# Decay attention and a sticky-routed MoE on Trainium2: two q loads, one low half of weights and the token gathers change places

## The chip, the cores and the metric

The kernel runs on one core of one Trainium2 chip. The metric is the device time of one execution in microseconds (us); the time of a kernel is the median of its runs. One more execution was taken by the hardware profiler, and all rows below come from that one.

## The reference, cut to what matters

Attention with a decay, 8 batches of 8 heads, 576 positions, 64 wide, and then a mixture of 8 experts in which a token either takes its own best expert or keeps the expert of the token before it.

```
def _attn_ref(q, k, v, f):                      # B, H, S, D = 8, 8, 576, 64
    scores = scale * np.matmul(q, k.transpose(0, 1, 3, 2))
    cum = np.cumsum(np.log(np.clip(f, 0.0001, 1.0)), axis=-1)
    decay = cum[:, :, :, None] - cum[:, :, None, :]
    scores = np.where(causal, -1000000000.0, scores + decay)
    attn = softmax(scores)
    return np.matmul(attn, v)

def _moe_ref(x, w_gate, w_local, w1, w2):       # x: 8 x 576 x 512, w1: 8 x 512 x 1024, w2: 8 x 1024 x 512
...
            fresh_e = int(np.argmax(logits[b, s]))
            e = fresh_e if s == 0 or local_gate[b, s] < 0.5 else prev_e
...
            h = np.maximum(x[b, s] @ w1[e], 0.0)
            out[b, s] = p[e] * (h @ w2[e])
```

All is float32. The kernel multiplies in fp16 with each operand split into a high and a low half (x = high + low), and three products in place of one: high by high, high by low, low by high.

## The kernel before, in words

**Engines.** TensorE (PE) multiplies, VectorE (DVE) and ScalarE (ACT) read its results from PSUM and split them, GpSimd (POOL) splits inputs, adds weights and issues the transfers with lists of indices (gathers and scatters), SyncE (SP) issues all other transfers, in the order of the program. Each engine works its instructions off in order.

**Attention.** Eight batches come one after the other, each in 25 units of up to 512 columns. A unit is: scores st on PE (L894, a product over 128 partitions of Ak and Aq and one over 70 of KB and QB, the latter carrying the decay), the negated maximum nm on DVE (L905), the exponentials P on ACT (L925), transposes pt of P on PE (L940), their high half ph on ACT (L945) and low half pl on DVE (L949), and the product with v on PE (xp, L919). Four heads' columns are divided by their sums at L980 (reciprocal rs) and L984.

While a batch is computed, the next ones are prepared. SP loads q and k into ldq and ldk (load_main, L209: two transfers of 512 KB for each; load_last, L216: the last 64 positions). POOL splits them to fp16, t16q and t16k (hi_lo, L359 the high, L363 the low half), PE turns the pieces (L429, 8 at a time), ACT or DVE write them to Aq or Ak, and SP copies the other half of each into QB and KB (L409 and L406, the last 64 positions at L413). What is issued when is set by lists of moves at the head of the file: each list has a due time of a planner, and when it is reached, its moves are issued in the order that they stand in. ORDC holds two lists, due at 47000 and 56000 of the planner's time:

```
ORDC = moves_of("q:2"), moves_of("k:2 q:L k:L")
...
        elif a == "2":
            new_load(2, b)
            for C in range(2):
                load_main(2, b, C, 0, H)
        elif a == "L":
            load_last(2, b)
```

The copies KB<-Ak of the second batch stand between the two on SP's queue.

**MoE.** Two fixed stages of experts come first, then six ranked stages r = 0 to 5 (the function `ranked`, and the loop that calls it), which take the experts by their number of tokens, with room for 608, 592, 576, 576, 544 and 480. A stage is a sequence of steps, and a list of (step, function) pairs says beside which step of PE everything else is issued. Steps 0 to 27 are W1 by seven products in place of eight (`seven`): products zb and zd (L1848), a kept copy et on ACT (L1855), sums y and zd on DVE (L1861), then the high half hh on ACT (L1865) and the low half hl on DVE (L1866). From step 28 on come the tiles of W2, four steps each, 24 matmuls of 512 columns (L1805). Where more than 64 tokens are left over 128s (96 in r=0 and r=5, 80 in r=1), that tile is turned: its 96 matmuls are as narrow as its tokens (L1800), and it comes second, in r=5 first; a smaller rest is a half tile at the end (L1809). Each tile's result is multiplied by the gate into a tile o of three buffers on ACT (L1748; a half tile at L1776) and scattered by POOL (L1750), with a drain of POOL ahead of the scatter (L1749).

Beside these steps stand, among others:
- the second half of the weights of the stage's own expert, cut into high halves on ACT (L2118: uh, or wh where the buffer has that name) and low halves on DVE (L2120: ul, wl), at the steps in the table UC, a pair (high, low) for each 128 rows;
- the sums of the next expert's weights on POOL (L2132 to L2141);
- the loads of the expert after it on SP, as buffers come free (L2090, L2093);
- the tokens of stage r+2, for r = 0 to 3: gathers xg<-xs of 128 tokens each on POOL (L1695) at the first step of XA, and their transposes xT<-xg on SP (L1700) at the second.

```
UC = (0, 0), (1, 1), (2, 2), (22, 23), (24, 25), (26, 27)
XA = (32, 42)
...
        todo += [call(y, M.second, (i + 2) // 2, i % 2, low) for i, x in enumerate(UC) for low, y in enumerate(x)]
...
            todo += tokens_at(r + 2, XA)
```

Of the kernel before, what the change touches and what calls it, by code (L numbers as in the profile page):

```python
# [38 lines left out]
def moves_of(d):  # L39
    return [tuple(x.split(":")) for x in d.split()]  # L40
# [5 lines left out]
ORD2 = moves_of(':lm q:M k:m k:M :sp :at 0:R 1:R :lv q:a k:a')  # L46
ORDA = moves_of("q0:P k:M 0:V 1:V k:ag")
ORDB = moves_of("q:ag q:G0 2:V q1:P k0:P k1:P 3:V q:G1 k:G0 :vl :Vl k:G1 :iv v0:P")
ORDC = moves_of("q:2"), moves_of("k:2 q:L k:L")


LI = (16, 18)
# [46 lines left out]
SEVEN = (1, 1, 1, 1, 1, 1)  # L99
WP = (28, 30, 32, 36)  # L100
LA = (6, 7, 8, 9), (10, 11, 12, 13)
UC = (0, 0), (1, 1), (2, 2), (22, 23), (24, 25), (26, 27)
UB = 45
UN = (5, 24, 29)
XA = (32, 42)
WC = (28, 29, 29, 30, 31, 31, 38, 38)
TA = (28, 36, 37, 44)
FA = (9, 10, 11, 12, 13, 14, 15, 16), (17, 18, 19, 20), (1, 4, 7, 9), (17, 22), (15, 16, 17, 18), 22, (20, 26)
# [8 lines left out]
def kernel(  # L117
# [586 lines left out]
    def due_c(i):  # L704
        for x in ORDC[i]:
            moves(x)
# [1795 lines left out]
    def call(x, f, *args):  # L2502
        return x, lambda: f(*args)
# [13 lines left out]
    def tokens_at(r, at):  # L2517
        if r >= NR:
            return []

        def gathers():
            Xs[r] = tokens_of(r)
            whole(both(*Xs[r][1]))

        return [(at[0], gathers), (at[1], lambda: whole(both(*Xs[r][2])))]
# [17 lines left out]
    for r in range(NR):  # L2543
        M, xc, todo = N, xn, []
        todo += [call(y, M.second, (i + 2) // 2, i % 2, low) for i, x in enumerate(UC) for low, y in enumerate(x)]
        if r + 1 < NR:
# [3 lines left out]
            todo += [call(0, N.load, ST)] + [call(x, N.load) for x in UN]  # L2550
            todo += tokens_at(r + 2, XA)
            if SEVEN[r + 1]:
# [100 lines left out]
```

## Time and profile before

| | us |
|---|---|
| median of 3 runs | 783.45 |
| runs, lowest to highest | 780.44 to 786.8 |
| the profiled execution, its own time | 784.89 |
| its span | 783.1 |
| PE busy in it | 738.4 |

The mean granted clock of PE over the span is 0.989 of full speed. A group's rows say: the start in us from the span's start, how long it took, engine, line, operation, what is written and from what, shapes, and how many instructions the row stands for; in brackets how long the engine stood idle before it, and what ended that. "issue" there means that the engine waited for nothing that the profile shows. SPq is SP's queue of transfers issued. Rows of a window give, for a stretch, the busy time and count of each engine, the granted clock, the busy share of the DMA engines and what they moved.

### The profile page before, as it was taken

Reading aid. Unit: us, or ns where it says so; the run is one execution under the profiler, and the core shown is the slowest. Engines: PE = TensorE matmul, PEld = TensorE weight load, DVE = VectorE, ACT = ScalarE, POOL = GpSimd, SP = SyncE. Lnnn points to the kernel's source line nnn. Section 1 sums busy time; section 2 is a strip of 40 time slices with the busy share of each in tenths; the row PEclk is TensorE's granted clock in tenths of the full one; section 3 lists DMA queues with packets and bytes.
Section 4 is the critical chain, followed back from the end, with each engine's and each line's share of the span. In section 5 each row is a group of like instructions: output and inputs, shape, how many; then the busy total and the mean of one; then the engine's idle time right before and its main releaser. Section 6 shows DMA issues by size and latency. Waiting matters only on the chain.

```text
span 783.1 us, 21924 instructions
## 1 busy us (share of the span) xinstructions
PE 738.4 (94%) x8661; PEld 537.7 (69%) x8661; DVE 599.3 (77%) x1295; ACT 508.3 (65%) x1006; POOL 469.0 (60%) x521
## 2 busy tenths in 40 slices
PE   5898999999999998989799999999999999999996
PEld 3686888887878877878554565575664747576682
DVE  7886888898898989899648856669577695968650
ACT  7796788988878978868524315366464665657441
POOL 6879969395879849837672365436282553634201
PEclk9999999999999999999999999999999999999999
DMA  7559879798786968155794776497737486561201
GB/s 186 139 124 201 177 160 185 168 148 208 149 188 129 177 155 154 37 98 192 179 244 154 189 198 119 116 237 155 232 102 163 151 178 209 151 224 64 73 3 50
DMA packets 189659, 120.75 MB, mean 154 GB/s; under 512 B 129397, under 2 KB 165511, under 8 KB 189532
## 3 DMA queue, kind: packets, MB, share of 16 engines
q1 hardware_dynamic: 183473, 100.19, 55.4%
q0 software_dynamic: 6080, 19.13, 8.1%
q8 instruction: 69, 1.13, 0.6%
q14 instruction: 37, 0.30, 0.1%
HBM read 72.25 MB, written 19.32 MB: 117 GB/s over the span
## 4 chain that ended last, share of the span: by engine, by line
PE 61%; DVE 12%; issue 12%; ACT 6%; POOL 4%; POOLq 2%; DMA 1%; ACTq 0%; DVEq 0%
PE y L1805 15%; PE pt L940 9%; PE st L894 7%; PE xp L919 6%; PE z L1763 6%; PE zb L1848 5%; DVE nm L905 4%; DVE pl L949 3%; PE st L429 3%; POOLq L1749 2%; PE zd L1848 2%; ACT ph L945 2%; ACT P L925 2%; PE yt L1848 1%; PE y L1800 1%
## 5 line engine op out<-in xcount | busy, mean ns | idle before, releaser
L925 ACT ACTIVATE P<-st,nm 128x512 f32<-128x512 f32 (+3 forms) x288 | 152.8, 588 | 27.6 <-DVE nm L905 25.5
L945 ACT CAST ph<-pt 128x512 f16<-128x512 f32 (+1 forms) x200 | 115.4, 588 | 38.1 <-PE pt L940 35.1
L905 DVE TENSOR_REDUCE nm<-st 128x1 f32<-128x512 f32 (+4 forms) x264 | 133.1, 540 | 7.2 <-PE st L901 4.7
L949 DVE TENSOR_TENSOR pl<-pt,ph 128x512 f16<-128x512 f32 (+1 forms) x165 | 109.1, 668 | 24.8 <-ACT ph L945 22.6
L940 PE MATMUL pt<-ident,P 128*128 128x128 f32 x784 | 121.9, 281 | 5.0 <-DVE pl L949 2.1
L1750 POOL DMA_INDIRECT out_dram<-o,ranki x26 | 30.2, 1162 | 135.4 <-ACT o L1748 59.3
L940 PEld LDWEIGHTS pt<-ident,P 128*128 128x128 f32 x784 | 84.3, 142 | 21.3 <-DVE pl L949 3.7
L919 PE MATMUL xp<-VH,pl 128*128 128x65 f16 (+1 forms) x960 | 90.2, 195 | 6.3 <-DVE pl L949 5.7
L919 PE MATMUL xp<-VH,ph 128*128 128x65 f16 (+1 forms) x960 | 91.6, 196 | 3.0 <-ACT ph L945 2.0
L919 PEld LDWEIGHTS <-ph 128*128 128x128 f16 (+1 forms) x1920 | 83.8, 103 | 11.7 <-issue 4.5
L1805 PEld LDWEIGHTS <-hh 128*128 128x128 f16 x528 | 51.4, 98 | 58.5
L919 PE MATMUL xp<-VL,ph 128*128 128x65 f16 (+1 forms) x960 | 91.0, 195 | 0.0
L894 PE MATMUL st<-Ak,Aq 128*128 128x256 f16 (+4 forms) x448 | 77.6, 284 | 4.4 <-ACT P L925 2.4
L919 PEld LDWEIGHTS <-pl 128*128 128x128 f16 (+1 forms) x960 | 75.4, 103 | 7.6 <-DVE pl L949 6.7
L894 PE MATMUL st<-KB,QB 70*128 70x256 f16 (+4 forms) x448 | 77.1, 280 | 2.2 <-DMA KB<-Ak 2.2
L1805 PE MATMUL y<-uh,hh 128*128 128x512 f16 x168 | 63.7, 379 | 0.0
L1805 PE MATMUL y<-uh,hl 128*128 128x512 f16 x168 | 63.7, 379 | 0.0
L1805 PE MATMUL y<-ul,hh 128*128 128x512 f16 x168 | 63.7, 379 | 0.0
L1763 PE MATMUL z<-xT,wh 128*128 128x384 f16 (+2 forms) x256 | 55.8, 309 | 1.0 <-DVE hl L1738 0.9
L1805 PEld LDWEIGHTS <-hl 128*128 128x128 f16 x264 | 25.8, 98 | 30.7
L1848 PEld LDWEIGHTS <-wh 128*128 128x128 f16 x384 | 37.5, 98 | 10.9 <-issue 2.5
L1748 ACT ACTIVATE o<-y,rank 128x512 f32<-128x512 f32 x23 | 15.7, 683 | 44.1 <-PE y L1805 31.4
(441 smaller groups left out, 2014.0 us busy)
## 6 DMA issues: line engine op xcount, KB each, us to landing
stg<-in_moe_w_dram SPq DMA_DIRECT2D x64, 512.0 KB
xs<-xr SPq DMA_DIRECT2D x16, 512.0 KB
ldq<-in_q_dram SPq DMA_DIRECT2D x14, 512.0 KB
ldk<-in_k_dram SPq DMA_DIRECT2D x14, 512.0 KB
ldv<-in_v_dram SPq DMA_DIRECT2D x28, 256.0 KB
QB<-Aq SPq DMA_DIRECT2D x15, 256.0 KB
KB<-Ak SPq DMA_DIRECT2D x15, 256.0 KB
ldv<-in_v_dram SPq DMA_DIRECT2D x20, 64.0 KB
```

The costliest lines, as they stand in the source:

```text
L429: nc.tensor.transpose(U["pt"][:, a], t16[:, 8 * j + a], ident16)
L894: nc.tensor.matmul(st[p0:p0 + m, co:co + n], lhsT=queries(lq, kk, h, c), rhs=rhs, start=(ps == 0 and first and co == col), stop=(ps == 1), ...
L905: nc.vector.tensor_reduce(dst, src, axis=AX.X, op=ALU.max, negate=True)
L919: nc.tensor.matmul(xo, lhsT=a[:, c0:c0 + m], rhs=w[:, vi, :], start=False, stop=(i == n - 1 and jj == 2), skip_group_check=True)
L925: nc.scalar.activation(P[:, c0:c1].rearrange("p (k x r) -> p k r x", r=2, x=64), st[:, c0:c1].rearrange("p (k r x) -> p k r x", r=2, x=64) ...
L940: nc.tensor.matmul(U["pt"][:, i * 128:(i + 1) * 128], lhsT=P[:, i * 128:(i + 1) * 128], rhs=ident, is_transpose=True, start=(i == 0), stop ...
L945: nc.scalar.copy(U["ph"][:, :cols], U["pt"][:, :cols])
L949: nc.vector.tensor_tensor(U["pl"][:, :cols], U["pt"][:, :cols], U["ph"][:, :cols], ALU.subtract)
L1750: nc.gpsimd.indirect_dma_start(out=outf if EX.get("over") else next_out(), out_offset=bass.IndirectOffsetOnAxis(ap=scat(t)[0:m], axis=0), ...
L1763: nc.tensor.matmul(z[:, a, 0:wd], lhsT=w[:, d, fc * 128:(fc + 1) * 128], rhs=xT[:, x, a * wd:(a + 1) * wd], start=(i == 0), stop=(i == len ...
L1805: nc.tensor.matmul(y[0:m], lhsT=a[:, fc, t * 128:t * 128 + m], rhs=u[:, fc], start=(i == 0), stop=(i == len(prods) - 1))
L1848: nc.tensor.matmul(out, lhsT=w, rhs=v, start=(start and i == 0), stop=(i == len(ops) - 1), skip_group_check=True)
```

## The change

Three lines of tables:

```
-ORDC = moves_of("q:2"), moves_of("k:2 q:L k:L")
+ORDC = moves_of(""), moves_of("q:2 k:2 q:L k:L")
...
-UC = (0, 0), (1, 1), (2, 2), (22, 23), (24, 25), (26, 27)
+UC = (0, 0), (1, 1), (2, 2), (22, 24), (24, 25), (26, 27)
...
-XA = (32, 42)
+XA = (37, 44)
```

The first moves the loads of q of the third batch from the list of 47000 to the head of the list of 56000. On SP, in the attention of the first batch, this stands in the program (QB and KB are the second batch's):

```order
 L409 DMA QB_109<-Aq 64x2x1024 x2
 L413 DMA QB_109<-Aq 64x512
-L209 DMA ldq<-in_q_dram 128x8x128 x2
 L406 DMA KB_111<-Ak 64x2048 x2
 L413 DMA KB_111<-Ak 64x512
+L209 DMA ldq<-in_q_dram 128x8x128 x2
 L209 DMA ldk<-in_k_dram 128x8x128 x2
 L216 DMA ldq<-in_q_dram 64x4x64 x2
```

The two loads of q went behind three copies of k; nothing else on SP changed place.

The second moves one low half (L2120, the fourth pair of UC) by one step in each ranked stage. On DVE, in stage r=1, near the end of W1:

```order
 L1866 SCALAR_TENSOR_TENSOR hl<-zb,hh 128x296
 L1866 SCALAR_TENSOR_TENSOR hl<-yt,hh 128x296
-L2120 SCALAR_TENSOR_TENSOR ul<-stg,uh 128x512
 L1861 TENSOR_TENSOR y<-zd,et 128x296
+L2120 SCALAR_TENSOR_TENSOR ul<-stg,uh 128x512
 L1861 TENSOR_TENSOR zd<-zd,et 128x296
 L1866 SCALAR_TENSOR_TENSOR hl<-y,hh 128x296
```

The low half went behind the first of two sums; the other five stages read alike, with other widths.

The third moves the gathers of stages 0 to 3 from step 32 to step 37, and their transposes from step 42 to step 44. On POOL, in stage r=0 (s and stg are the sums of the next expert's weights, out_dram the scatters):

```order
 L2136 TENSOR_TENSOR s_11172<-stg 128x512
 L2141 TENSOR_TENSOR s_11186<-stg,s_11172 128x512 x2
+L1750 DMA out_dram<-o,ranki 4608x512
 L1695 DMA xg<-xs,ranki 128x1024 x4
 L1695 DMA xg<-xs,ranki 64x1024
-L1750 DMA out_dram<-o,ranki 4608x512 x5
+L1750 DMA out_dram<-o,ranki 4608x512 x4
 L2132 TENSOR_TENSOR stg<-stg 128x512
 L2136 TENSOR_TENSOR s_11727<-stg 128x512
```

The first of the stage's five scatters now stands ahead of the five gathers. Among SP's transfers the transposes keep their place, and the instructions of PE and ACT stand in the same order as before.

## Rows read from the trace of the kernel before

**Rows 1.** The page's list of busy time: engine, us, share, instructions.
```profile
PE 738.4 (94%) x8661; PEld 537.7 (69%) x8661; DVE 599.3 (77%) x1295; ACT 508.3 (65%) x1006; POOL 469.0 (60%) x521
```

**Rows 2.** Timeline of PE, at the wait for KB and at the turns of q.
```profile
69.01 0.38 PE L894 MATMUL st<-KB,QB 70*128 70x512 f16 x1 [2.22 <-DMA KB<-Ak]
...
86.23 2.17 PE L429 MATMUL st<-ident,t16q 128*128 128x128 f16 x36
```

**Rows 3.** Timeline of SP's queue, 57 to 67 us.
```profile
57.99 2.08 SPq L209 DMA_DIRECT2D ldq<-in_q_dram  x2
60.90 3.60 SPq L406 DMA_DIRECT2D KB<-Ak  x2
...
65.19 1.33 SPq L209 DMA_DIRECT2D ldk<-in_k_dram  x2
```

**Rows 4.** Windows: us, PE, PEld, DVE, ACT, POOL busy (count), PEclk, DMA share, GB/s.
```profile
57.00:60.50 3.50, 3.50 (x71) 3.00 (x68) 3.06 (x9) 2.44 (x6) 3.42 (x4) 1.00 0.94 185
...
69.00:73.60 4.60, 4.59 (x73) 3.79 (x73) 2.20 (x5) 2.43 (x5) 4.51 (x6) 0.63 1.02 204
```

**Rows 5.** Timeline of DVE, 67 to 74 us.
```profile
67.06 1.02 DVE L949 TENSOR_TENSOR pl<-pt,ph 128x512 f16<-128x512 f32 x2 [1.86 <-ACT ph L945]
...
73.61 0.18 DVE L980 RECIPROCAL rs<-xp 128x4 f32<-128x4 f32 x1 [1.35 <-PE xp L919]
```

**Rows 6.** Timeline of POOL, 74 to 84 us.
```profile
74.34 1.04 POOL L359 TENSOR_SCALAR t16q<-ldq 128x1024 f16<-128x1024 f32 x1
75.47 2.28 POOL L363 TENSOR_TENSOR t16q<-ldq,t16q 128x512 f16<-128x512 f32 x2
...
80.08 2.77 POOL L363 TENSOR_TENSOR t16q<-ldq,t16q 128x640 f16<-128x640 f32 x2
...
83.94 1.04 POOL L359 TENSOR_SCALAR t16k<-ldk 128x1024 f16<-128x1024 f32 x1
```

**Rows 7.** PE's waits, 505 to 783 us: total, times, longest; the whole list.
```profile
PE y L1800 <- issue: 2.4, 6, 0.5
PE zd L1848 <- DVE y L1861: 1.7, 4, 0.6
PE y L1800 <- DVE hl L1866: 0.2, 1, 0.2
```

**Rows 8.** Timeline of all engines near the end of W1, stage r=1.
```profile
576.69 1.79 DVE L2120 SCALAR_TENSOR_TENSOR ul<-stg,uh 128x512 f16<-128x512 f32 x1
...
576.88 0.41 ACT L1855 COPY et<-zb 128x296 f32<-128x296 f32 x1 [0.21 <-PE zb L1848]
...
578.41 0.46 DVE L1861 TENSOR_TENSOR y<-zd,et 128x296 f32<-128x296 f32 x1
...
578.92 0.41 PE L1848 MATMUL zd<-xT,wh 128*128 128x296 f16 x2 [0.57 <-DVE y L1861]
```

**Rows 9.** Timeline of DVE, the same low half in stage r=5.
```profile
753.79 0.69 DVE L2120 SCALAR_TENSOR_TENSOR ul<-stg,uh 128x512 f16<-128x512 f32 x1
```

**Rows 10.** Windows of L1800 alone (r=0, 1, 5): PE, PEld, PEclk, DMA share, GB/s.
```profile
535.49:541.82 6.33, 4.75 (x96) 4.27 (x95) 1.00 0.70 235
584.85:589.68 4.83, 3.92 (x96) 3.58 (x95) 1.00 1.09 252
755.48:760.00 4.52, 4.27 (x96) 4.16 (x95) 1.00 0.02 4
```

**Rows 11.** Timeline of PE in the turned tile of r=0.
```profile
538.88 0.33 PE L1800 MATMUL y<-hh,wl 128*128 128x96 f16 x4 [0.48 <-issue]
539.60 0.33 PE L1800 MATMUL y<-hl,wh 128*128 128x96 f16 x4 [0.39 <-issue]
```

**Rows 12.** Timeline of POOL in stage r=0: gathers, then scatters.
```profile
534.61 1.26 POOL L1695 DMA_INDIRECT xg<-xs,ranki  x1
...
540.38 1.92 POOL L1695 DMA_INDIRECT xg<-xs,ranki  x1 [0.30 <-issue]
549.47 1.02 POOL L1750 DMA_INDIRECT out_dram<-o,ranki  x1 [7.17 <-issue]
553.21 0.98 POOL L1750 DMA_INDIRECT out_dram<-o,ranki  x1 [2.73 <-issue]
```

**Rows 13.** Timeline of ACT in stage r=0: first and last o, next et.
```profile
538.06 0.67 ACT L1748 ACTIVATE o<-y,rank 128x512 f32<-128x512 f32 x1
...
558.05 0.69 ACT L1748 ACTIVATE o<-y,rank 128x512 f32<-128x512 f32 x1 [4.49 <-PE y L1805]
558.75 0.41 ACT L1855 COPY et<-zb 128x296 f32<-128x296 f32 x1
```

## The prediction

> **What bounds the kernel now.** I read the page's list of busy time first: TensorE (PE) is busy 738.4 us of a span of 783.1 [rows 1], so an edit pays only where it removes PE idle time or slow clock, and little more than 40 us of idle time is there to remove. Next I read the list of what PE waits for, once in the attention part and once over the six ranked stages, then the timelines around those waits.
>
> At 69.01 PE stands still for 2.22 us, the longest wait in its neighbourhood, for the copy KB<-Ak [rows 2]. The copy was issued at 60.90, but behind it on the wires were two loads of q for the third batch (ldq, issued from 57.99, 512 KB each) [rows 3], and in that stretch the transfers already filled 0.94 of the DMA engines [rows 4]. After the wait, from 69.00 to 73.60, the mean granted clock is 0.63, so PE, busy 4.59 of 4.60 us, does that work partly at the lower of its two levels [rows 4].
>
> In the ranked stages the whole list of PE's waits is three lines: 2.4 us in six waits of the turned tile (L1800) for nothing the profile shows ("issue"), 1.7 us in four waits of a W1 product (L1848) for VectorE's y (L1861), and 0.2 us for hl [rows 7]. The three edits aim at the first wait of attention and at the first two lines of this list.
>
> **First edit: q loads of the third batch go behind the copies of k.** Nothing is added or removed; on SyncE (SP) two 512 KB loads move past two KB copies and the small last one. The copies were issued as soon as Ak was written and then shared the wires with 1 MB. Alone, 256 KB at the 185 GB/s of [rows 4] take 1.4 us, so an estimate for their landing is 63 to 65, before PE wants KB at 66.79 (69.01 less 2.22). Gone with it should be the 2.22 us, and of the slow stretch (1 - 0.63) x 4.6 = 1.7 us, 3.9 in all for PE alone.
> Two caps make it less. VectorE ends its pl at 68.08 and has 2.20 us of work before the reciprocal of 73.61 [rows 4, 5], so that unit can't end before 70.3: 3.3 us earlier at most. And the 36 turns of q at 86.23 [rows 2] need the low half of t16q, which GpSimd (POOL) ends at 80.08 + 2.77 = 82.85 [rows 6]: 3.4 at most. POOL has no idle time there, so this second cap doesn't move unless something delays POOL.
> What is queued later: ldq is now issued around 65.2 in place of ldk [rows 3], so 1 MB at 204 GB/s [rows 4], 5.1 us, lands near 70.5, if ldk takes its share near 72. POOL wants ldq at 74.34 and ldk at 83.94 [rows 6]; the margin is 2 to 4 us. I take 3.3 us saved. Bounds: 3.9 saved; or none, and 1 lost, if ldq lands at 75.3 and POOL passes that on.
>
> **Second edit: one low half of W2 a step later, in all six stages.** On VectorE the 512-element L2120 changes place with the first of the two L1861 adds. In stage r=1 L2120 ran from 576.69 for 1.79 us, although et, which the add needs, was there at 577.29 (576.88 + 0.41); the add came at 578.41, and PE waited 0.57 us for it [rows 8]. With the new order the add starts at about 577.3, and PE, which was free at 578.35, doesn't wait. The four waits are 1.7 us in sum, so 1.7 is the cap.
> Against it: VectorE now stands idle until et is there, and L2120 and the hl behind it come later by that idle time, 0.5 us. In stage r=5, where L2120 takes only 0.69 us [rows 9] and there was no wait for y, the hl is read at once by the turned tile, where PE already waits 0.2 [rows 7]: I take 0.3 lost there, 1.4 saved in all. Bounds: 1.7 saved, 0.5 lost if each hl is late. The moved low half issues no DMA, since all eight loads of its expert are out by then.
>
> **Third edit: token gathers behind the turned tile.** Five gathers of stage r=0 (L1695, five or four in the next three) move on POOL past the first scatter (L1750); the transposes on SP stay where they were among SP's transfers. In r=0 the turned tile takes 6.33 us, of which PE is busy 4.75; in r=5, which gathers nothing, the same 96 matmuls take 4.52 and are busy 4.27 [rows 10]. The holes of 0.3 to 0.5 us come while gathers run (534.61 to 542.30) [rows 11, 12]. The loss is 6.33 - 4.27 = 2.1 in r=0, and in r=1 with 80 of 96 columns 4.83 - 4.27 x 80 / 96 = 1.3: 3.3 us. The gathers of r=2 and r=3 run beside ordinary 512-column tiles and cause no wait of PE: the list names L1805 nowhere [rows 7]. If the holes belong to the meeting of gathers and the short matmuls, all 3.3 go, for the gathers now wait for the first o, 538.06 + 0.67 = 538.73 [rows 13], and its scatter of 1.0 us, and the tile would end at 535.49 + 4.3 = 539.8.
> The Trainium skill, "Runtime: NRT & Kernel Launch", section "Instruction fetch mechanics", says that each engine's sequencer fetches its own instructions in blocks ahead of time and that this is hidden behind issue. By it the holes could hardly be a starved fetch, and the gain would be 0, as in the first rival; here the holes do exist, beside heavy transfers, and the trace can't show what the sequencer waited for.
> What it costs: every later scatter of the stage now stands behind the gathers and the drain ahead of a scatter. The gathers take 7.7 us, so from 540.0 they end at 547.7; the drain behind them lasted 7.17 before the first scatter [rows 12], which gives 554.9 for the second scatter in place of 553.21, and with 1.0 us and an estimated 2 for landing 558. The tile o has three buffers, so the fifth o of the stage, at 558.05 less the 2.1 saved, 556, needs that landing [rows 13]; ScalarE is in order, and the et of the next W1 step is directly behind it (558.75). So at worst 2 us in r=0. Much of the 7.17 was beside a weight load that is over by then; I take 0.7 over the four stages, so 2.6 saved. Bounds: 3.3 saved; 8 lost at 2 in each stage with no gain against it.
>
> **Sum.** 3.3 + 1.4 + 2.6 = 7.3 us. The profiled execution took 784.89 us (span 783.1): 777.6. The median of the runs shown, 783.45, is 1.4 lower, well inside their spread of 780.44 to 786.8, so I leave the number there and lengthen the range downwards.
>
> **Rivals.**
> *The holes of the turned tile stay.* A weight load is on the wires in the same stretch and isn't moved, or the holes go wherever the short matmuls are. For it: the DMA share is 0.70 and 1.09 there against 0.02 in r=5 [rows 10], and that isn't gathers alone. Then the third edit gives -0.7 instead of 2.6 and the sum is 4.0: 780.9.
> *The q load is late.* ldq and ldk are issued within 3 us and share the wires; if ldq lands after 74.34, t16q, the turns of q and the end of the batch move with it and the first edit's 3.3 is lost: 780.9 with the other two, 784.2 if the holes stay as well. Against it stands a margin of 2 to 4 us.
> *Scatters too late: slower.* One mechanism: in r=0 to 3 the second scatter waits for gathers and drain, holds the o buffer, and so ScalarE's et and PE at each stage's end. If each gather lasts as long as the last one, 1.92 + 0.30 us [rows 12], five take 11.1 us from 540.0, the drain 7.17, scatter and landing 3: 561.3, 5.3 after the o is wanted; with the shorter estimate above it is 2. At 3.5 in each of four stages, 14 us, less the 3.3 + 1.4 + 3.3 of the other terms: 790.9. It outweighs them from 2 us a stage. Against it: in the kernel before, too, the second scatter comes behind gathers and drain, and only 1.7 us earlier than 554.9 (553.21).
> Beside this rival stands a rule of the Trainium skill, "SBUF — State Buffer", section "SBUF: two separate sides": while VectorE runs an operation that holds the port pair it shares with GpSimd, a transfer issued by GpSimd can't get its descriptors written. In the trace a gather takes between 1.26 and 1.92 us, and VectorE's L2120 1.79 in one place and 0.69 in another [rows 8, 9, 12], as such a lock would have it, but no row names the cause; the price above uses only the durations.
>
> **How the numbers follow.** All three terms as summed: 0.38. Holes stay: 0.26. The q load late, or its gain lost further on in attention: 0.20. Scatters too late: 0.07. What is left, 0.09, is an end near 784 where small losses eat the gains. So 777.6 is the likeliest. Low end: all caps, 3.4 + 1.7 + 3.3 = 8.4, give 776.5, and runs of one kernel lie up to 4.4 under the profiled one: 772.5. High end: 784.5, which takes in 784.2 and leaves the slower rival out. About 1%, 7.8 us, is what a measurement of this kernel can tell from no change. The forecast's 7.3 lies just under it, so some 0.28 falls to faster, most to no change, and the slower rival gives 0.07.
>
> **What would show it.** Right: no wait of PE for KB near 67 and a granted clock of 1.0 behind it; the reciprocal near 70.3 and the q turns near 83; t16q still at 74.3; no line "zd <- y" in PE's list; the turned tile at 4.3 and 3.6 us in r=0 and r=1. Wrong: t16q after 74.5 with an idle POOL ahead of it (first edit); holes in L1800 as before (third); a wait of ScalarE's last o for a transfer, then PE for et or y, at the ends of r=0 to 3 (the slower rival); a longer wait for hl in r=5 (second).

## The result, and the profile after

The changed kernel takes 791.79 us (median of 6 runs, 787.28 to 796.11) where the kernel before takes 783.36 (6 runs): a ratio of 1.0135 with a 95% interval of 1.009 to 1.0181, slower by 7 to 14 us. 777.6 was forecast, in a range that ended at 784.5. The profiled execution took 790.96 us, 6.1 more than the one of before.

TensorE's list of waits over the ranked stages (total, times, longest) tells most of it:

```profile
PE zb L1848 <- ACT et L1855: 10.3, 4, 3.9
PE y L1800 <- DVE hl L1866: 0.5, 1, 0.5
PE y L1805 <- DVE wl L2120: 0.2, 1, 0.2
```

The two lines at which the second and third edit aimed, 2.4 and 1.7 us in [rows 7], are gone. In their place stands a wait that wasn't in that list, four times et, 10.3 us. To see where et was, one reads ScalarE, then POOL, then TensorE at the end of stage r=0 (timelines: start, us):

```profile
557.17 0.69 ACT L1748 ACTIVATE o<-y,rank 128x512 f32<-128x512 f32 x1 [8.83 <-DMA out_dram<-o,ranki]
557.76 0.40 ACT L1855 COPY et<-zb 128x296 f32<-128x296 f32 x1
```

```profile
535.32 1.12 POOL L1750 DMA_INDIRECT out_dram<-o,ranki  x1 [4.55 <-ACT o L1748]
536.74 1.96 POOL L1695 DMA_INDIRECT xg<-xs,ranki  x1 [0.30 <-issue]
...
544.03 0.96 POOL L1695 DMA_INDIRECT xg<-xs,ranki  x1 [0.30 <-issue]
553.25 0.99 POOL L1750 DMA_INDIRECT out_dram<-o,ranki  x1 [8.25 <-issue]
```

```profile
558.20 0.41 PE L1848 MATMUL zb<-th,uh 128*128 128x296 f16 x1 [3.95 <-ACT et L1855]
```

The second scatter starts at 553.25, behind the gathers and 8.25 us of drain; it has landed, and the o buffer is free, at about 557.17; ScalarE, which has stood idle for 8.83 us (4.49 in the kernel before, for y [rows 13]), writes o, and only then et, for which TensorE has waited 3.95. The other three stages have 2.4, 1.9 and 1.9 us in the same place.

The waits aren't their whole price. Behind the first two of the four, the granted clock falls to its lower level (windows as in [rows 4]):

```profile
558.20:561.60 3.40, 3.40 (x14) 2.08 (x14) 2.58 (x5) 2.24 (x5) 0.85 (x1) 0.51 0.99 313
609.40:612.80 3.40, 3.40 (x17) 2.10 (x15) 2.47 (x5) 1.43 (x4) 0.00 (x0) 0.51 0.98 357
```

At (1 - 0.51) x 3.4 = 1.7 us each, an estimate, that is 3.3 us more.

The first edit's story is in TensorE's timeline, with SP's queue beside it:

```profile
64.93 0.38 PE L894 MATMUL st<-KB,QB 70*128 70x512 f16 x1
...
108.24 0.38 PE L894 MATMUL st<-Ak,Aq 128*128 128x512 f16 x1
...
114.01 0.59 PE L894 MATMUL st<-KB,QB 70*128 70x512 f16 x1 [5.38 <-DMA KB<-Ak]
...
117.05 0.63 PE L894 MATMUL st<-KB,QB 70*128 70x256 f16 x2
```

```profile
59.20 3.60 SPq L406 DMA_DIRECT2D KB<-Ak  x2
...
63.49 1.34 SPq L209 DMA_DIRECT2D ldq<-in_q_dram  x2
...
99.19 1.04 SPq L209 DMA_DIRECT2D ldq<-in_q_dram  x2
...
102.82 2.07 SPq L209 DMA_DIRECT2D ldk<-in_k_dram  x2
...
107.35 2.33 SPq L406 DMA_DIRECT2D KB<-Ak  x2
```

At 64.93 there is no wait for KB any more, where 2.22 us stood at 69.01 [rows 2]. The third batch begins at 108.24. In the kernel before the same two matmuls stand here:

```profile
113.66 0.38 PE L894 MATMUL st<-Ak,Aq 128*128 128x512 f16 x1
113.87 0.38 PE L894 MATMUL st<-KB,QB 70*128 70x512 f16 x1
...
115.48 0.39 PE L894 MATMUL st<-KB,QB 70*128 70x256 f16 x2
```

So TensorE was 5.4 us ahead (1.7 of it from before this place: the copy KB<-Ak was issued at 59.20 and 60.90), and then stands 5.38 us for the next copy KB<-Ak. That copy was issued at 107.35, behind four loads of 512 KB for the fourth batch (issued from 99.19 to 104.9) and its small last ones (L216, to 107.2). The windows of the changed kernel (us; PE, PEld, DVE, ACT, POOL busy; clock; DMA share; GB/s) show the DMA engines' share at 1.0 or above through all of it:

```profile
99.00:108.00 9.00, 9.00 (x179) 7.63 (x175) 7.29 (x19) 7.31 (x14) 7.15 (x33) 1.00 1.00 244
108.60:114.00 5.40, 0.02 (x1) 0.00 (x0) 0.67 (x2) 0.81 (x2) 5.23 (x6) 0.73 1.26 197
114.00:118.00 4.00, 3.99 (x32) 2.98 (x33) 2.60 (x7) 1.87 (x5) 3.92 (x5) 0.51 0.99 167
```

After the standstill the granted clock is 0.51, its lower level, and so a matmul of 0.38 us takes 0.59. The last of the pairs above is 1.6 us behind before (117.05 against 115.48): 5.4 ahead became 1.6 behind, and with the 1.7 that were there already taken off, the first edit has cost 3.3 us between these two executions.

### The profile page after: what moved, and what is told of

Its sections match the earlier page's. It is cut to its first block, busy times and chain, and to the rows that moved or that the text cites. A ratio compares the mean times of both kernels' runs of the same rounds, so it can differ in the third digit from the quotient of the medians.

```text
span 789.2 us, 21923 instructions
## 1 busy us (share of the span) xinstructions
PE 736.3 (93%) x8661; PEld 535.1 (68%) x8661; DVE 598.2 (76%) x1295; ACT 508.0 (64%) x1006; POOL 470.3 (60%) x521
## 4 chain that ended last, share of the span: by engine, by line
PE 36%; issue 18%; DVE 13%; POOL 11%; POOLq 5%; ACT 5%; DMA 2%; SPq 1%; ACTq 0%; DVEq 0%
PE pt L940 7%; PE z L1763 6%; PE st L894 6%; PE xp L919 5%; PE y L1805 5%; POOLq L1749 4%; DVE nm L905 4%; DVE pl L949 3%; POOL xg L1695 2%; POOL s L2141 2%; PE st L429 2%; POOL s L2136 2%; POOL stg L2132 2%; ACT ph L945 1%; ACT P L925 1%
## 5 line engine op out<-in xcount | busy, mean ns | idle before, releaser
L940 PE MATMUL pt<-ident,P 128*128 128x128 f32 x784 | 120.2, 279 | 6.0 <-DVE pl L949 3.2
L1750 POOL DMA_INDIRECT out_dram<-o,ranki x26 | 28.5, 1095 | 143.2 <-ACT o L1748 68.8
L919 PE MATMUL xp<-VH,pl 128*128 128x65 f16 (+1 forms) x960 | 89.3, 194 | 6.0 <-DVE pl L949 5.3
L919 PE MATMUL xp<-VH,ph 128*128 128x65 f16 (+1 forms) x960 | 91.0, 195 | 2.0 <-ACT ph L945 2.0
L919 PE MATMUL xp<-VL,ph 128*128 128x65 f16 (+1 forms) x960 | 90.4, 194 | 0.0
L919 PEld LDWEIGHTS <-ph 128*128 128x128 f16 (+1 forms) x1920 | 83.1, 102 | 10.4 <-issue 3.2
L919 PEld LDWEIGHTS <-pl 128*128 128x128 f16 (+1 forms) x960 | 74.7, 102 | 7.4 <-DVE pl L949 6.4
```

Source lines behind the costliest of these rows:

```text
L919: nc.tensor.matmul(xo, lhsT=a[:, c0:c0 + m], rhs=w[:, vi, :], start=False, stop=(i == n - 1 and jj == 2), skip_group_check=True)
L940: nc.tensor.matmul(U["pt"][:, i * 128:(i + 1) * 128], lhsT=P[:, i * 128:(i + 1) * 128], rhs=ident, is_transpose=True, start=(i == 0), stop ...
L1750: nc.gpsimd.indirect_dma_start(out=outf if EX.get("over") else next_out(), out_offset=bass.IndirectOffsetOnAxis(ap=scat(t)[0:m], axis=0), ...
```

## The experiments

All times of the kernel before lie between 773.43 and 791.69 us beside these experiments, so a single run says little. What counts are the ratios to the kernel before, each with its 95% interval in brackets, and the waits in the traces, one profiled execution for each kernel.

**The parts alone.** First edit alone:

```
+ORDC = moves_of(""), moves_of("q:2 k:2 q:L k:L")
```

> Only the first edit: the q loads of the third batch behind the copies of k. Theory (a wait handed on by one batch): TensorE's wait for KB at the start of the second batch (2.2 us, with a half clock behind it) goes, the second batch ends some 3.7 us earlier on TensorE, and then the third batch's copy KB<-Ak meets the loads of the fourth batch, so that a wait for KB of about 5 us at 108 to 114 and half clock behind it take all of it back and more: 3 to 4 us slower than before at the end of attention. Rival (the first edit keeps its gain, and the whole loss is the gathers'): no wait for KB at either place, about 3.5 us faster than before.

Ratio 1.0129 (1.0037 to 1.0222), from four runs: 3 to 17 us, where 3 to 4 were expected. From the list of TensorE's waits, 60 to 120 us:

```profile
PE st L894 <- DMA KB<-Ak: 5.4, 1, 5.4
```

The line is the wait of the third batch; the one of the second is gone. The first edit loses by itself, and the rival falls. The wait of the third batch stands in all three profiles that have the first edit without a further change to SP's loads (5.4 here and in the change, 3.0 in one below), and in none of the nine in which q's loads were not put later. In this execution the holes of the turned tile don't appear, though the gathers stand where they stood.

Second edit alone:

```
+UC = (0, 0), (1, 1), (2, 2), (22, 24), (24, 25), (26, 27)
```

> Only the second edit: one low half of W2 a step later. Theory: the four waits of zd for y (1.7 us) go and nothing takes their place but a wait for hl of 0.5 in place of 0.2 us in the last stage, 1.0 to 1.5 us faster, within what can't be told from no change. Rival (the low half is now late for the tile behind it): a wait of y for ul or wl in several stages, 1 to 3 us slower.

Ratio 0.996 (0.9905 to 1.0016): no difference that can be told, on the forecast side. Its whole list over the ranked stages:

```profile
PE zb L1848 <- ACT et L1855: 2.7, 2, 1.6
PE y L1800 <- DVE hl L1866: 0.5, 1, 0.5
```

No wait of zd for y, and hl at 0.5 us, as expected; no wait for ul or wl. But there is a wait for et here too, with the gathers at their old place, and again no holes.

Third edit alone:

```
+XA = (37, 44)
```

> Only the third edit: gathers at step 37, behind the first scatter. Theory (o buffers): the holes of the turned tile go (3.3 us less), and in each of the first four stages ScalarE's last o waits for the scatter that stands behind gathers and drain, and TensorE for et behind it: 10 us in four waits, 6 to 8 us slower than before in sum. Rival (the et waits come from the low half that the second edit moved, together with the gathers): fewer than 2 us of et waits, 1 to 3 us faster.

Ratio 1.0105 (1.0016 to 1.0193). The four et waits are there in the same stages, without the second edit:

```profile
PE zb L1848 <- ACT et L1855: 10.6, 4, 4.4
PE zd L1848 <- DVE y L1861: 0.5, 1, 0.5
PE y L1800 <- DVE hl L1866: 0.2, 1, 0.2
```

The theory's 10 us and its place are right, and the rival (the low half) falls.

**Which of the gathers' neighbours makes the wait.** The gathers still later, behind three scatters:

```
+XA = (45, 47)
```

> Gathers at step 45 and transposes at step 47, behind the first three scatters; the rest as before. Theory (o buffers): the scatters whose buffers the last o of a stage needs are issued ahead of the gathers, so the four et waits (10 us) are gone, the holes of the turned tile too, 2 to 4 us faster than before, unless the transposes and the weight loads behind them are now late. Rival (the waits at the stage's end come from the gathers' traffic on the wires, wherever they stand): et waits or o waits for a DMA of some 10 us stay, 5 us or more slower than before.

Ratio 0.9973 (0.9926 to 1.002), and TensorE's list has no line for et; a new one of 2.0 us in two waits for ScalarE's o to empty y stands in its place. POOL's timeline in r=0:

```profile
535.36 1.68 POOL L1750 DMA_INDIRECT out_dram<-o,ranki  x1 [5.78 <-ACT o L1748]
541.38 1.82 POOL L1750 DMA_INDIRECT out_dram<-o,ranki  x1 [4.35 <-ACT o L1748]
545.95 1.37 POOL L1750 DMA_INDIRECT out_dram<-o,ranki  x1 [2.74 <-ACT uh L2118]
547.62 1.01 POOL L1695 DMA_INDIRECT xg<-xs,ranki  x1 [0.30 <-issue]
...
558.99 1.02 POOL L1750 DMA_INDIRECT out_dram<-o,ranki  x1 [5.36 <-ACT hh L1865]
```

The scatter that the last o needs starts at 541.38 instead of 553.25. The gathers' traffic is the same and lies nearer to the stage's end, so it isn't what held et. The gain, some 2 us, is at the low end of the 2 to 4 expected, and the interval holds 1, so that it isn't shown.

Four o tiles, gathers as in the change:

```
-            o = (EX["oe"] if op is ep else op).tile([128, DM], F32, name="o", bufs=6 if op is ep else 3)
+            o = (EX["oe"] if op is ep else op).tile([128, DM], F32, name="o", bufs=6 if op is ep else 4)
...
-            o = op.tile([128, DM], F32, name="o", bufs=3)
+            o = op.tile([128, DM], F32, name="o", bufs=4)
...
-            return EX["fx"].tile([128, 304], F32, name="et", bufs=5)[:, 0:n]
+            return EX["fx"].tile([128, 304], F32, name="et", bufs=3)[:, 0:n]
...
+XA = (37, 44)
```

> The third edit alone with four o tiles in place of three; for their room the kept copies et have three buffers in place of five. Theory (o buffers): the last o of a stage then needs only the first scatter, which stands ahead of the gathers, so ScalarE's waits for out_dram and TensorE's 10 us of et waits behind them go; some waits of W1 for et may come from the smaller pool. Rival (the drain or the wires, not the buffers): the four waits of 2 to 4 us stay.

One run, 778.59 us. Its whole list over the ranked stages:

```profile
PE y L1805 <- ACT o L1748: 5.1, 3, 2.3
PE zd L1848 <- DVE y L1861: 0.5, 1, 0.5
PE y L1800 <- DVE hl L1866: 0.2, 1, 0.2
```

Same order on POOL as in the third edit alone, one buffer more, and all four et waits are gone; the smaller pool of et can't have helped. Two experiments from two sides, then, show the chain gathers, drain, scatter, o buffer, et. The 5.1 us for y are new; which of the two sizes changed makes them wasn't tried apart.

**Were the holes the kernel's?** The kernel before, profiled once more:

> The kernel before, unchanged, profiled once more. Theory (the holes belonged to one execution): the unexplained waits of the turned tile (2.4 us in six) and the two beside the early gathers (1.0 us) aren't there, and without them the last o of a stage comes too late by itself: 2 to 3 us of TensorE's waits for et appear, as in the two kernels that left the gathers where they were. Rival (the holes are the kernel's own, and the first and second edit somehow removed them): the same six waits of 2.4 us in sum, no wait for et.

One run, 783.74 us. The list over the ranked stages:

```profile
PE zb L1848 <- ACT et L1855: 7.9, 2, 4.2
PE y L1800 <- DVE hl L1866: 0.3, 1, 0.3
PE zd L1848 <- DVE y L1861: 0.2, 1, 0.2
```

The same program, and no hole, only 0.2 us of waits for y, and 7.9 us of waits for et, more than expected. (The two other holes that the expectation names, 1.0 us at L919 near 387 us, are gone as well.) Nor does this execution wait for KB in the second batch; its second batch ended as early as with the first edit, and the third waited for nothing: its loads for the fourth batch had gone out from 95.53, not 99.19, and its copy from 105.36, not 107.35. Against this execution the first edit cost more than the 3.3 us above: from the first product with KB of the second batch to the last of the rows shown there it took 45.1 us (66.03 to 111.09), in the change 52.1. Over all executions profiled, the holes of the turned tile stand in 2 of 7 with the gathers at step 32 (before, and the change with its gathers put back), and in none of 6 with later gathers. So they may have to do with the gathers, but they aren't in most executions, and 2 in 7 leaves chance open. Waits for et stand in 6 of those 7, 2.2 to 7.9 us: so the kernel before was at the edge of this wait already, and the profile that I read was the one of the seven that didn't show it. The wait for KB in the second batch, 2.0 to 2.4 us, stands in 6 of 8 executions with the q loads where they were; in the seventh it is 0.4 us, in the eighth nothing. And the waits of zd for y, 1.7 us in the profile that I read, are 0.2 to 1.7 us in the 8 executions without the second edit, 0.8 on average.

**Where the first edit's gain went.** The first edit, and the loads of the fourth batch's k behind the third batch's copies KB<-Ak:

```
-            for nm, i in ("q", LI[0]), ("k", LI[1]):
-                bulk.append((i, lambda nm=nm: nm in done, lambda nm=nm: (new_load(b + 1, nm), load_main(b + 1, nm, 0, 0, H))))
+            for nm, i in ("q", LI[0]), ("k", LI[1] if b != 2 else -2):
+                bulk.append((i, lambda nm=nm: nm in done and (b != 2 or nm == "q" or (2, "k", 3) in turned), lambda nm=nm: (new_load(b + 1, nm), load_main(b + 1, nm, 0, 0, H))))
```

> The first edit, and the load of the fourth batch's k moved behind the third batch's copies KB<-Ak. Theory (the copies meet the loads of the fourth batch): the wait of 5.4 us for KB near 108 to 114 shrinks to under 2 us, and at the end of attention the kernel stands 2 to 3 us ahead of before, not 3 to 4 behind. Rival (the copy is late by itself, because its batch came earlier): the wait stays at 5 us.

Ratio 1.0004 (0.9964 to 1.0044). There is no wait for KB at all, neither in the second nor in the third batch: the copies did meet the loads. The expected gain didn't come all the same. POOL waits, its routing work for the expert choice (eq, L1395) is late, VectorE stands in order behind it, and TensorE with it (POOL, VectorE, TensorE):

```profile
133.74 1.04 POOL L359 TENSOR_SCALAR t16k<-ldk 128x1024 f16<-128x1024 f32 x1 [12.63 <-PE pt L940]
```

```profile
151.77 0.24 DVE L1397 TENSOR_REDUCE F<-eq 128x10 f32<-128x80 f32 x1 [2.98 <-POOL eq L1395]
```

```profile
152.66 0.66 PE L940 MATMUL pt<-ident,P 128*128 128x128 f32 x4 [2.64 <-DVE pl L949]
```

The k loads were now issued at 126.02, and POOL split them from 133.74 on, after 12.63 us of idle time; the row's releaser is a matmul that t16k doesn't read, so that it was the late loads is argued from the times, not shown. What is shown is that the gain was gone one batch further on: the reciprocal of [rows 5] stands 3.7 us ahead of before in the third batch (118.98 against 122.65), and in the fourth only 0.4 (159.22 against 159.65). Moving q the other way:

```
-('c0', 47000)
+('c0', 40000)
```

> The q loads of the third batch moved the other way: ahead of the copies of q (due at 40000 in place of 47000). Theory: 1 MB is on the wires some 4 us earlier, the copies of k of the second batch meet less of it, and the wait for KB at 64 to 69 shrinks from 2.2 us to under 1; the loads of the fourth batch aren't pushed back, so the third batch's wait for KB stays under 3 us; 0 to 3 us faster. Rival (any earlier end of the second batch only moves the wait to the next): 4 to 5 us of wait for KB near 108, 0 to 3 us slower.

Ratio 1.0008 (0.996 to 1.0056): no change. The wait for KB of the second batch stays at 2.5 us, for the loads came out only 5.1 us ahead of the copies (55.13 and 60.22) where 2.9 stood before (57.99 and 60.90 in [rows 3]), and the theory's price for it was wrong; in the third batch there is no wait for KB, as it expected.

**Sums.** The change with its gathers put back, `XA = (32, 42)`:

> The change with the gathers put back to step 32 (first and second edit together). Theory: the wait for KB of 5.4 us in the third batch stays, et waits fall to the 3 to 8 us of the kernel before; 2 to 5 us slower than before. Rival (the gathers are the whole loss): the same as before or faster.

Ratio 1.0055 (1.002 to 1.0091), some 4.3 us. The third batch's wait for KB is 3.0 us here. Of the ranked stages its list begins with:

```profile
PE y L1800 <- issue: 2.6, 6, 0.5
PE zb L1848 <- ACT et L1855: 2.2, 1, 2.2
```

The change with its q loads put back, `ORDC` as before:

> The change with the q loads put back (second and third edit together). Theory: et waits of 10 us in four stages, each with a chance of half clock behind it, the wait for KB of the second batch as before; 5 to 9 us slower than before. Rival (the q loads are the larger loss): 0 to 3 us slower.

Ratio 1.0101 (1.0031 to 1.0171), some 7.9 us, with the same 10.3 us of et waits. The second edit is in both. Counted as nothing it leaves 12.2 for the three, and counted at its own -3.1 (0.996) 15.3, where the change measured 10.6 (7 to 14): the parts add up within what their intervals allow. By the traces the gathers are the larger loss: 10.3 to 10.6 us of et waits in each of the three profiles with them at step 37 and three o tiles, against 0 to 7.9 (3.5 on average) in the seven with them at step 32; and behind one, two and three of the four waits there stands a stretch of 3.4 us or more at the lower clock.

The two small gains together, q loads as before:

```
+UC = (0, 0), (1, 1), (2, 2), (22, 24), (24, 25), (26, 27)
+XA = (45, 47)
```

> The q loads as before, the second edit, and the gathers at step 45 and the transposes at step 47. Theory (o buffers; no hole was a property of the kernel): no wait for et at the ends of the first four stages, no wait of zd for y, the wait for KB of the second batch in most executions as before; 3 to 6 us faster than before, the two small gains of the single runs together. Rival (those two medians were chance): the same as before within 2 us.

Ratio 0.9967 (0.9932 to 1.0001), 2.6 us less than before, with 0.8 us of et waits left and none for y. It is faster than the change, whose interval begins at 1.009, and against before its interval just reaches no difference, so it isn't shown to beat it.

## Why the prediction was wrong

**First edit: the step that failed is "What is queued later".** The removal was right: no wait for KB at 64.93, no half clock there, and the reciprocal of 73.61 [rows 5] stands at 68.23, 3.7 us earlier when the 1.7 of the start are taken off, against a cap of 3.3. POOL took ldq at 72.49 and was held up 0.73 us by the last positions at 76.63, nothing more. What I asked of the later loads was only when POOL needs them. I didn't follow SP's queue on to the next copies of the same kind. SP had no slack there (in the changed kernel its queue has no gap over 0.1 us from 88.6 to 109.7): its loads for the fourth batch went out 1.6 us later (99.19 against 97.63), TensorE came 5.4 us earlier, and the copy that TensorE wants next, KB<-Ak, came to stand behind 2 MB of loads. I had this only as half a sentence of a rival ("or its gain lost further on in attention"), and priced it as a gain of nothing, not as a loss of 3.3 with a half clock behind it.

**Second edit: right in its mechanism.** The waits for y are gone in all five profiles that have it, and hl rose from 0.2 to 0.5 us as forecast; 1.4 us were forecast, and the runs can't resolve them (0.996, 0.9905 to 1.0016). The 1.7 us that the term starts from was the most that any of eight executions showed; from their average of 0.8, less the 0.3 taken off for hl, it would be 0.5.

**Third edit: two steps failed.** First, "3.3 us" of holes were read off one execution, and there too large: 4.27 is a busy time set against a whole duration, and the list of waits has 2.4 [rows 7, 10]. The waits with "issue" as their releaser had no cause in the profile, and they weren't in the next execution of the same program, so most executions had nothing of the kind to give. The loss of the turned tile in the changed kernel (532.52 to 536.77) is nil, as forecast; it was nil in five of seven executions without the edit as well.

Second, "I take 0.7 over the four stages": the mechanism was written down, with its place, and mis-sized; 10.3 us of waits came, with some 3.3 of slow clock behind them, for which the sum has no term. In r=0 the chain from the first scatter's o to the free buffer was put at 19.3 us (538.7 to 558), some 2 us too late "at worst", and took 22.1 (535.04 to 557.17): the gathers 8.25 us for 7.7, the drain 8.25 for 7.17, the second scatter with its landing 3.9 for 1.0 and "an estimated 2". TensorE waited 3.95. The 2 was then reduced because much of the drain was "beside a weight load that is over by then". SP's queue in the kernel before shows otherwise:

```profile
529.11 6.39 SPq L2093 DMA_DIRECT2D stg<-in_moe_w_dram  x2
539.38 10.07 SPq L1700 DMA_TRANSPOSE xT<-xg  x5
```

The last weight load was issued by 535.5, 6.8 us before the drain began (542.3 to 549.47). What was issued beside the drain are the transposes of the gathered tokens, and they go with the gathers: in the changed kernel they are issued from 541.16 to 554.21, the drain lies between 545.0 and 553.25. For the other three stages there was no working at all. Their drains were shorter (5.3, 5.0 and 4.4 us), their landings took 4.8, 3.1 and 4.5, and TensorE waited 2.4, 1.9 and 1.9.

**The slower rival** had this mechanism, its place and its four stages, at 3.5 us each, and 7 in 100; it came with 2.6 on average, over the 2 from which it was to outweigh all other gains, and those didn't come. That its 790.9 lies near the 791.79 measured is luck: it has 14 us of waits less 8 of gains, and knows neither the loss of the first edit nor the slow clock.

Two slips bear on nothing: 776.5 less 4.4 is 772.1, not 772.5, and the five gathers of [rows 12] took 0.98 to 1.92 us each, not 1.26 to 1.92.

The Trainium skill, "Runtime: NRT & Kernel Launch", "Instruction fetch mechanics", was set against the holes: by it the fetch of instructions is mostly hidden. Most executions agree with it (11 of 13 profiles have no wait of the turned tile for nothing), and what the other two waited for stays open. The Trainium skill, "Perfetto Trace Analysis", "DMA Instruction — HWDGE (DVE, Sync)", warns that a transfer's completion can come surprisingly late when it writes to HBM; that section is on transfers of another path, but the scatters here, which write to HBM through POOL, took 3.1 to 4.8 us from start to release, 4.1 on average, and I had put 3.

What stays open: whether the holes depend on where the gathers stand, what sets the drain behind gathers (4.4 to 8.3 us in the changed kernel), and why the wait for KB is missing or 0.4 us in 2 of 8 executions.

## What to carry to other kernels

When a wait goes, ask who comes earlier and follow the queue on to the next transfer of the same kind; where the queue has no slack, the wait is handed on. Ask also for the clock behind a wait: here some standstills of 2 to 5 us had 3.4 us or more at the lower level behind them, and the sum has to have a term for it. A term that rests on idle time without a releaser needs a second profile of the same program before it is counted as a gain. Where an engine works in order, every instruction moved ahead of a scatter delays the buffer that the scatter frees, so count the buffers and the landing before the gain.

## What the runs showed of the hardware that was not expected

Two executions of one program differ in which waits they have: of the kernel before, one had 2.4 us of holes, 1.7 of waits for y, 2.2 for KB and none for et, the next no holes, 0.2 for y, none for KB and 7.9 for et, and their times, 784.89 and 783.74 us, are almost the same. The granted clock fell behind some standstills of TensorE and not behind others, and not by their length: in the changed kernel the waits for et of 3.95 and 2.44 us have 3.4 us at 0.51 behind them, the two of 1.94 none (1.00 in the four us behind each); with the third edit alone a wait of 3.36 us has none (1.00 from 608.4 to 611.8), and with the second and third one of 1.98 has it (0.51 from 706.2 to 709.6). Nor did the longest standstill (5.38 us) cost much more of it than the one of 2.22 us in the kernel before: 3.9 us at 0.50 (114.0 to 117.9) against some 3.4, from about 69.4 on (0.50 from 70 to 72, 0.58 from 72 to 73).
